# Another order for the first tile's jobs in an attention and SwiGLU kernel

## The chip, the cores and the metric

One core of a Trainium2 chip. The time is that of one execution on the device, in microseconds. The engines are TensorE (PE, matmuls; PEld its weight loads), VectorE (DVE), ScalarE (ACT), GpSimd (POOL), and SyncE (SP), which issues most DMAs; ACT issues the loads of the weights.

## The reference

Attention over 8 batches, 8 heads, 576 positions and head size 64, with keys and values first averaged over groups of 8 positions, then a gated feed-forward layer over all 4608 rows:

```python
k_p = k.reshape(B, H, Sp, 8, D).mean(axis=3)          # Sp = 72
v_p = v.reshape(B, H, Sp, 8, D).mean(axis=3)
scores = scale * np.matmul(q, k_p.transpose(0, 1, 3, 2))
attn = np.exp(scores - np.max(scores, axis=-1, keepdims=True))
attn = attn / (np.sum(attn, axis=-1, keepdims=True) + 1e-09)
x = np.matmul(attn, v_p)                               # then to (4608, 512)
g = x @ w_gate                                         # (512, 1536)
out = (g / (1 + np.exp(-g)) * (x @ w_val)) @ w_out     # (1536, 512)
```

All is float32; q and k are drawn with a spread of 0.8, v with 0.1.

## The kernel before

The 4608 rows are cut into 9 tiles of 512 rows, and the 1536 hidden columns into 12 chunks of 128. To keep float32 accuracy on 16-bit matmuls every operand is split into a high and a low part, and each product is three matmuls (lines 931 to 933). The weights come in 64-bit words, one DMA of 1536 KB for each chunk, and are unpacked and split on the chip once, while tile 0 is computed; after that they stay. Tiles 1 to 8 are run by a planner, which follows its own count of PE's time and puts pieces of attention for later tiles between the matmuls of the current one.

Tile 0 is different. Its work is a list of jobs, ORDER, one name for each, and `first_tile` calls them in that order:

```python
for name in ORDER.split():
    what = name.rstrip("0123456789")
    n = int(name[len(what) :] or 0)
    now["job"] = name
    jobs[what](n)
```

It stands in a manual schedule, so each engine runs its instructions in the order in which the list issues them, and one that waits holds up all behind it on its engine. The engines run beside each other; a job starts when its inputs are there. A DMA that ACT or SP issues is such an instruction too, and waits there until the buffer that it writes is free. The raw tiles (weight words, the first k, and later the "box" of batch 2 and up) share two buffers, and the loads of v, k and q of later batches share three.

The names, with a number for the chunk, piece, step or batch:

- A chunk c of weights: Lw (load, ACT's queue), c (abs, line 244) and b (sign, 231) on ACT, a (ends, 237) and d (join, 248) on DVE, e (sums, 259, ACT), f (total over rows, 209 and 210, PE), g (scale, DVE), h and j (high part of the gate and value weight, ACT; h0, h3 and j1 on POOL), i and k (their low parts, 282, DVE), l (output weight, ACT), m (its low part, 291, POOL), un (factors, POOL).
- Keys and values of batch 0 and 1: Lk, Lv, Lr, Lu (loads, SP), Kp (DVE), Kb and Kq (POOL) sum keys over 8 positions; Vp and Vq sum values (420, PE); Vm, Vo, Vs, Vx, Vh, Vg, Vf scale and split them.
- A piece p of up to 128 rows of attention (0 to 3 are tile 0, 4 to 8 tile 1): Lq (load q), S (scores, 629, PE), M (less the largest, 645 and 646, DVE), E (exponential, 653, ACT), Na (one over the sums, 674 on, DVE), N (normalise, 683, POOL), H and P (high and low part, 696 on ACT, 702 and 703 on POOL), T (a DMA transpose on SP), Y (times values, 747 to 750, PE), R (scale factors, 911 on, DVE), X and Z (high and low part of the rows of x, 770 on ACT and 774 on DVE).
- A hidden step k: G and V (gate and value product, PE), t (tanh, 945, ACT), u and v (949 and 955, DVE), w (copy, 1283, ACT), y (low part, 1287, DVE), O (product with the output weight into the accumulators, 967, PE). Steps 0 to 2 are chunks 0 to 2 for the first 256 rows, 3 to 5 the same chunks for the other 256, and from step 6 on step k is chunk k - 3 for all 512 rows.
- La and Pa: loads and sums for batch 2 (POOL for Pa0 to Pa3, DVE for Pa4 to Pa7).
- ZERO opens the four accumulators with one matmul of zeros each (1246). D with a number issues that many more matmuls of zeros into the first accumulator (1250), I with a number as many into a bank of the gate and value products (1255). They add nothing to the result.

After the list comes O14, the last step's output product, then tile 0 is stored and tile 1 begins.

Of the kernel before, what the change touches and what calls it, by code (L numbers as in the profile page):

```python
# [34 lines left out]


ORDER = """
Lw0 Lk0 Lk1 Lq0 Lv0 Lv2 Kp0 Lv1 Lq1 c0 Kb0 b0 Lu0 a0 CZ Kp1 S0 Lr0 d0 Lq2 M0 l0 Lw1 Vp0
Vp2 E0 Na0 S1 I2 Kq0 e0 f0 Vp1 N0 M1 m0 c1 g0 h0 Vm0 j0 E1 Lq3 Vo0 k0 Vs0 Lu2 I4 H0 Na1
Vx0 Vh0 Vq0 R0 P0 Lr1 Vg0 N1 un0 I5 S2 M2 i0 S3 T0 Kq1 Lu1 H1 Vf0 E2 Y0 Na2 Vq2 X0 Lw2  # L40
Z0 P1 Vq1 b1 M3 Lq4 N2 Vm1 ZERO T1 Vo1 a1 d1 H2 E3 D10 Lw3 Vs1 P2 Vx1 l1 D6 Y1 Vg1 e1 T2
X1 Vh1 m1 R1 c2 f1 D14 g1 Z1 Na3 S4 b2 h1 Lq5 G0 a2 c3 i1 j1 b3 d2 un1 M4 V0 t0 Y2 u0 k1
l2 G1 v0 Lw4 X2 w0 y0 m2 e2 N3 t1 E4 a3 d3 H3 Z2 V1 D8 u1 Lw5 P3 f2 g2 v1 e3 f3 l3 O0 T3
h2 w1 g3 j2 un2 Lq6 c4 i2 G2 y1 m3 k2 j3 V2 h3 b4 t2 i3 Y3 O1 k3 c5 b5 a4 u2 X3 d4 v2 Z3
G3 w2 Vf1 y2 Lw6 V3 t3 O2 a5 d5 u3 v3 e4 f4 l5 Lw7 un3 g4 w3 y3 G4 j4 e5 V4 f5 Na4 O3 k4
t4 h4 c6 u4 v4 w4 N4 g5 l4 S5 y4 G5 m5 i4 M5 H4 b6 t5 u5 V5 v5 O4 P4 G6 Lq7 h5 T4 un4 a6
d6 m4 w5 c7 Lq8 S6 y5 E5 j5 l6 M6 e6 O5 V6 Lw8 Na5 un5 m6 N5 i5 t6 b7 u6 k5 f6 E6 G7 v6
H5 P5 w6 g6 t7 c8 y6 Na6 T5 j6 u7 S7 b8 un6 V7 M7 G8 h6 v7 E7 a7 w7 d7 y7 a8 Y4 Lw9 d8
O6 X4 N6 O7 i6 l7 t8 Z4 e7 Lw10 Y5 e8 V8 k6 X5 l8 m8 u8 m7 c9 Z5 f7 f8 v8 G9 g7 w8 g8
Na7 y8 b9 j7 a9 j8 h7 t9 un7 V9 u9 N7 O8 v9 i7 h8 w9 k7 c10 d9 G10 H7 y9 k8 un8 i8 V10  # L50
La0 t10 e9 f9 l9 u10 O9 v10 m9 P7 g9 Lw11 w10 un9 b10 y10 h9 j9 La1 O10 Pa0 i9 k9 a10
c11 G11 V11 d10 t11 G12 T7 l10 H6 u11 e10 v11 w11 b11 m10 y11 f10 O11 a11 g10 h10 t12
d11 La2 V12 j10 e11 u12 f11 i10 k10 l11 v12 P6 w12 m11 un10 G13 y12 t13 T6 g11 u13 j11
h11 k11 S8 La3 O12 M8 Pa2 un11 i11 La4 V13 E8 Y6 G14 Na8 v13 w13 y13 V14 N8 t14 H8 Ln
Pa3 P8 X6 Pa4 La5 u14 v14 Z6 w14 O13 T8 Y7 X7 Y8 y14 Pa5 Z7 X8 La7 La6 Z8 Pa6 Pa1 Pa7 A
A
"""
HIGH_ON_POOL = ('h0', 'h3', 'j1')
TILE = 512
# [1540 lines left out]
```

## Time and profile before

| | |
|---|---|
| median of 3 runs (lowest, highest) | 938.03 us (937.7, 938.47) |
| span of the profiled execution | 937.0 us |
| PE busy | 901.5 us, 96% |
| DVE busy | 642.8 us, 69% |
| ACT busy | 533.2 us, 57% |
| POOL busy | 439.7 us, 47% |
| first matmul | 11.27 us |
| tile 1's first matmul | 169.58 us |
| weight loads | 12 of 1536 KB, median 6.9 us from issue to landing |

Times of the profile count from the start of the span; 1.0 us of the median lies around it. A matmul's busy time includes its way through the array, so matmuls overlap, and how closely PE is filled is read from the distances between their starts: 0.22 us for one of 512 columns. A row of the timeline has start, duration, engine, line, operation, output and input, shapes and count, and in brackets how long the engine sat idle before it and what released it.

### The profile page before, as it was taken

What the parts mean: (1) busy time and instruction counts of PE and PEld (TensorE: products, weight loads), DVE (VectorE), ACT (ScalarE), POOL (GpSimd) and SP (SyncE); (2) the same over time, 40 slices, a digit from 0 to 9 for tenths busy, and PEclk for the clock granted to TensorE, in tenths of its full rate; (3) what the DMA queues carried; (4) which work ended last, traced back from release to release, by engine and by line L of the source; (5) the groups of instructions that cost most, each with busy time, mean ns of one, the idle gap of its engine ahead of it and who ended that gap; (6) DMA issues with size and microseconds to landing.
All of it is one profiled execution on the core that took longest, in us unless ns stands there. A gap on an engine that the chain in (4) does not pass through costs nothing.

```text
span 937.0 us, 17052 instructions
## 1 busy us (share of the span) xinstructions
PE 901.5 (96%) x6492; PEld 596.1 (64%) x6585; DVE 642.8 (69%) x1163; ACT 533.2 (57%) x1096; POOL 439.7 (47%) x509
## 2 busy tenths in 40 slices
PE   4899999999999999999999999999999999999997
PEld 3667545555445576467757775777577757777775
DVE  5888977886776768777776778667855585644233
ACT  2688774365555455657475655555556656444343
POOL 4654335388856754677366442543124317114111
PEclk9989999999999999999999999999999999999999
DMA  8965733356425633773356334652242321201001
GB/s 332 240 197 174 240 112 110 114 145 179 85 57 149 171 82 56 183 167 88 66 143 185 79 75 129 152 137 41 79 69 63 74 68 24 46 1 46 1 2 45
DMA packets 155538, 103.20 MB, mean 110 GB/s; under 512 B 113216, under 2 KB 141888, under 8 KB 153920
## 3 DMA queue, kind: packets, MB, share of 16 engines
q1 hardware_dynamic: 153728, 83.24, 36.1%
q10 hardware_dynamic: 1728, 18.88, 5.5%
q8 instruction: 51, 0.84, 0.4%
q14 instruction: 31, 0.25, 0.1%
HBM read 67.63 MB, written 9.44 MB: 82 GB/s over the span
## 4 chain that ended last, share of the span: by engine, by line
PE 81%; DVE 6%; DMA 4%; ACT 3%; POOL 3%; issue 2%; SPq 0%; ACTq 0%; DVEq 0%; POOLq 0%
PE gv L1115 29%; PE acc L967 26%; PE gv L931 7%; PE gv L932 7%; PE gv L933 7%; DMA ws<-w_all 2%; PE ps L635 1%; DVE ws L237 1%; PE ps L759 1%; PE ps L636 1%; ACT ws L231 1%; PE ps L760 1%; DMA in<-v_rest 1%; DMA pt<-area 1%; POOL fx L1070 1%
## 5 line engine op out<-in xcount | busy, mean ns | idle before, releaser
L1396 POOL TENSOR_TENSOR hl<-hf,hh 128x512 bf16<-128x512 f32 x71 | 93.2, 1312 | 202.3 <-ACT hh L1387 202.3
L945 ACT ACTIVATE hf<-gv,un 128x512 f32<-128x512 f32 (+1 forms) x111 | 74.8, 674 | 162.7 <-PE gv L1115 110.3
L967 PE MATMUL acc<-hl,wo_h 128*128 128x512 bf16 (+1 forms) x435 | 162.1, 374 | 2.3 <-issue 0.3
L949 DVE SCALAR_TENSOR_TENSOR hf<-hf,gv 128x512 f32<-128x512 f32 (+1 forms) x111 | 74.4, 670 | 115.1 <-ACT hf L945 114.7
L931 PE MATMUL gv<-x,wgv_h 128*128 128x512 f16 (+1 forms) x408 | 149.9, 367 | 1.6 <-ACT x L770 1.0
L932 PE MATMUL gv<-x,wgv_h 128*128 128x512 f16 (+1 forms) x408 | 149.8, 367 | 0.5 <-DVE x L774 0.5
L933 PE MATMUL gv<-x,wgv_l 128*128 128x512 f16 (+1 forms) x408 | 149.7, 367 | 0.0
L967 PE MATMUL acc<-hh,wo_h 128*128 128x512 f32 (+1 forms) x444 | 130.2, 415 | 0.0
L967 PE MATMUL acc<-hb,wo_l 128*128 128x512 bf16 x307 | 117.2, 382 | 0.4
L1115 PEld LDWEIGHTS <-mixed 128*128 128x128 f16 x1044 | 101.3, 98 | 25.5 <-issue 0.9
L618 POOL TENSOR_TENSOR box<-qt,box 64x512 f16<-64x512 f32 (+1 forms) x60 | 66.3, 1104 | 107.1 <-ACT box L617 93.6
L1115 PEld LDWEIGHTS <-wgv_h 128*128 128x128 f16 x960 | 92.9, 98 | 34.0 <-issue 2.1
L1387 ACT CAST hh<-hf 128x512 fp32r<-128x512 f32 x72 | 44.4, 617 | 119.8 <-DVE hf L955 119.8
L1115 PE MATMUL gv<-area,mixed 128*128 128x256 f16 x696 | 94.9, 273 | 0.0
L1115 PE MATMUL gv<-x,wgv_h 128*128 128x256 f16 x528 | 93.0, 273 | 0.0
L967 PEld LDWEIGHTS acc<-hh,wo_h 128*128 128x128 f32 x444 | 76.4, 190 | 13.7 <-ACT hh L1387 0.3
L955 DVE SCALAR_TENSOR_TENSOR hf<-gv,un,hf 128x512 f32<-128x512 f32 x72 | 53.8, 747 | 37.0 <-PE gv L1115 34.5
L967 PEld LDWEIGHTS <-wo_l 128*128 128x128 bf16 x444 | 43.4, 98 | 52.3 <-issue 25.4
L1115 PE MATMUL gv<-x,wgv_l 128*128 128x256 f16 x264 | 72.0, 273 | 0.0
L933 PEld LDWEIGHTS <-wgv_l 128*128 128x128 f16 x408 | 40.0, 98 | 43.8 <-issue 0.7
L932 PEld LDWEIGHTS <-wgv_h 128*128 128x128 f16 x408 | 40.0, 98 | 39.9 <-issue 2.0
L931 PEld LDWEIGHTS <-wgv_h 128*128 128x128 f16 x408 | 40.6, 99 | 38.5
(206 smaller groups left out, 1917.6 us busy)
## 6 DMA issues: line engine op xcount, KB each, us to landing
ws<-w_all ACTq DMA_DIRECT2D x12, 1536.0 KB, 6.9
qt<-q_twice SPq DMA_DIRECT2D x48, 256.0 KB, 3.0
out_t<-ob SPq DMA_DIRECT2D x36, 256.0 KB, 2.5
in<-k_rows SPq DMA_DIRECT2D x12, 576.0 KB, 5.0
in<-q_rows SPq DMA_DIRECT2D x12, 576.0 KB, 4.9
in<-v_main SPq DMA_DIRECT2D x12, 512.0 KB, 4.9
in<-v_rest SPq DMA_DIRECT2D x12, 512.0 KB, 4.8
qt<-q_rows SPq DMA_DIRECT2D x8, 256.0 KB, 6.4
```

What stands on the lines that cost most here:

```text
L231: nc.scalar.activation(high.bitcast(I32), high.bitcast(F32), AF.Prelu, scale=2.0**-18, alpha=2.0**90)
L618: nc.gpsimd.tensor_sub(o[rows], qt[rows], o[rows])
L931: nc.tensor.matmul(o, wh, x["h"][:, j, a:e], start=(j == 0), stop=False)
L932: nc.tensor.matmul(o, wh, x["l"][:, j, a:e], start=False, stop=False)
L933: nc.tensor.matmul(o, wl, x["h"][:, j, a:e], start=False, stop=(j == NJ - 1))
L945: nc.scalar.activation(hf, gate, AF.Tanh, scale=un[:, c, 0:1])
L949: nc.vector.scalar_tensor_tensor(out=hf, in0=hf, scalar=1.0, in1=gate, op0=ALU.add, op1=ALU.mult)
L955: nc.vector.scalar_tensor_tensor(out=out, in0=val, scalar=un[:, c, 2:3], in1=hf, op0=ALU.mult, op1=ALU.mult)
L967: nc.tensor.matmul(acc[j][:, a:e], w[:, c, j * P : (j + 1) * P], h[:, :n], start=begin and at < NJ, stop=end and w is wo_up,)
L1115: nc.tensor.matmul(o, a, b, start=begin and j + n == 0, stop=j == HJ - 1 and n == 2, skip_group_check=True,)
L1387: nc.scalar.copy(hh[:, :n], hf)
L1396: eng.tensor_sub(hl[:, :n], hf, hh[:, :n].bitcast(F32))
```

## The change

Only the list changes. All jobs but D6, D8, D10 and D14 are in it as before, in another order under the same dependencies and buffers; the four D jobs (38 zero matmuls) are left out, and ZERO and the three I jobs stay. Lines of the changed kernel are numbered two lower than before. The first and a later line of each list:

```diff
-Lw0 Lk0 Lk1 Lq0 Lv0 Lv2 Kp0 Lv1 Lq1 c0 Kb0 b0 Lu0 a0 CZ Kp1 S0 Lr0 d0 Lq2 M0 l0 Lw1 Vp0
...
-X1 Vh1 m1 R1 c2 f1 D14 g1 Z1 Na3 S4 b2 h1 Lq5 G0 a2 c3 i1 j1 b3 d2 un1 M4 V0 t0 Y2 u0 k1
+Lw0 c0 CZ Lk0 Lv0 Lk1 Vp0 Lq1 Kb0 Kp0 b0 Lw1 Kp1 Lq0 a0 S1 Lv2 S0 d0 Lv1 e0 Vp1 M1 f0 E1 M0 E0
...
+ZERO T2 S4 d2 b3 Kq0 M4 Lw4 e2 E4 l2 a3 un1 G0 m1 f2 Y3 j1 g2 V0 d3 t0 u0 X3 h2 Y2 i1 G1 j2 e3
```

Three places matter below. First, ScalarE's queue around the load of chunk 2 (L225 DMA, tile ws_386). Before, from V's scaling (L450) on:

```order
L450 ACTIVATE area_120<-ps_183,inv_122 64x4x64 x2
L696 CAST area_120<-sc_237 128x512
L698 CAST area_120<-sc_237 128x2x32 x2
L472 ACTIVATE area_120<-shapes_91,mask_92 128x2x64 x4
L653 ACTIVATE sc_323<-sc_323 128x576
L770 ACTIVATE x_289<-ps_355,r_296 128x4x128
L225 DMA ws_386<-w_all 128x3072
L231 ACTIVATE ws_181<-ws_181 128x1536
```

Now (there it is L223, tile ws_287), from chunk 1's abs (L242) and sign (L229) on:

```order
L242 ACTIVATE mixed_111<-ws_159 128x1536
L229 ACTIVATE ws_159<-ws_159 128x1536
L223 DMA ws_287<-w_all 128x3072
L448 ACTIVATE area_120<-ps_143,inv_122 64x4x64 x2
L694 CAST area_120<-sc_200 128x512
L696 CAST area_120<-sc_200 128x2x32 x2
```

The load has moved from behind the attention work of the first pieces, and ahead of chunk 1's sign, to right behind that sign.

Second, VectorE's queue around the first hidden step (u0 is L949 on hf_577, before; chunk 3's ends and join are L237 and L248 on ws_440):

```order
L949 SCALAR_TENSOR_TENSOR hf_577<-hf_577,gv0_537 128x256
L282 SCALAR_TENSOR_TENSOR wgv_l_108<-mixed_111,sw_514,wgv_h_107 128x512
L955 SCALAR_TENSOR_TENSOR gv1_564<-gv1_564,un_125,hf_577 128x256
L1287 TENSOR_TENSOR hl_618<-gv1_564,hh_616 128x256
L237 SCALAR_TENSOR_TENSOR ws_440<-ws_440 128x1536
L248 SCALAR_TENSOR_TENSOR mixed_111<-mixed_111,ws_440 128x1536
```

Now (u0 is L947 on hf_570, chunk 3 is ws_405):

```order
L235 SCALAR_TENSOR_TENSOR ws_405<-ws_405 128x1536
L213 TENSOR_SCALAR p2w_113<-ps_532 128x2
L216 RECIPROCAL sw_553<-p2w_113 128x2
L246 SCALAR_TENSOR_TENSOR mixed_111<-mixed_111,ws_405 128x1536
L947 SCALAR_TENSOR_TENSOR hf_570<-hf_570,gv0_518 128x256
L280 SCALAR_TENSOR_TENSOR wgv_l_108<-mixed_111,sw_438,wgv_h_107 128x512
L953 SCALAR_TENSOR_TENSOR gv1_556<-gv1_556,un_125,hf_570 128x256
```

Chunk 3's two long operations have moved from behind the first hidden step to ahead of it.

Third, GpSimd's queue around P6, the low part of piece 6 (L702 and L703 on half_123 from sc_1022, before), and the sums Pa of batch 2 (L301 to L303):

```order
L357 MEMSET box_1437 128x2x4x72
L301 TENSOR_TENSOR in_1381<-in_1381 128x2x256
L302 TENSOR_TENSOR in_1381<-in_1381 128x2x128
L303 TENSOR_TENSOR box_1437<-in_1381 128x128
L291 TENSOR_TENSOR wo_l_110<-mixed_111,wo_h_109 128x512
L702 TENSOR_TENSOR half_123<-sc_1022,half_123 128x512
```

Now, from Pa2 (in_776, the second of four) on:

```order
L299 TENSOR_TENSOR in_776<-in_776 128x2x256
L300 TENSOR_TENSOR in_776<-in_776 128x2x128
L301 TENSOR_TENSOR box_1413<-in_776 128x128
L299 TENSOR_TENSOR in_1058<-in_1058 128x2x256
L300 TENSOR_TENSOR in_1058<-in_1058 128x2x128
L301 TENSOR_TENSOR box_1413<-in_1058 128x128
L299 TENSOR_TENSOR in_1246<-in_1246 128x2x256
L300 TENSOR_TENSOR in_1246<-in_1246 128x2x128
L301 TENSOR_TENSOR box_1413<-in_1246 128x128
L700 TENSOR_TENSOR half_123<-sc_983,half_123 128x512
```

Three more of batch 2's sums have moved ahead of P6.

More of the change, by code (lines that the diff above doesn't have):

```diff
@@ L37 @@
 ORDER = """
-Lw0 Lk0 Lk1 Lq0 Lv0 Lv2 Kp0 Lv1 Lq1 c0 Kb0 b0 Lu0 a0 CZ Kp1 S0 Lr0 d0 Lq2 M0 l0 Lw1 Vp0
-Vp2 E0 Na0 S1 I2 Kq0 e0 f0 Vp1 N0 M1 m0 c1 g0 h0 Vm0 j0 E1 Lq3 Vo0 k0 Vs0 Lu2 I4 H0 Na1
-Vx0 Vh0 Vq0 R0 P0 Lr1 Vg0 N1 un0 I5 S2 M2 i0 S3 T0 Kq1 Lu1 H1 Vf0 E2 Y0 Na2 Vq2 X0 Lw2
-Z0 P1 Vq1 b1 M3 Lq4 N2 Vm1 ZERO T1 Vo1 a1 d1 H2 E3 D10 Lw3 Vs1 P2 Vx1 l1 D6 Y1 Vg1 e1 T2
-X1 Vh1 m1 R1 c2 f1 D14 g1 Z1 Na3 S4 b2 h1 Lq5 G0 a2 c3 i1 j1 b3 d2 un1 M4 V0 t0 Y2 u0 k1
-l2 G1 v0 Lw4 X2 w0 y0 m2 e2 N3 t1 E4 a3 d3 H3 Z2 V1 D8 u1 Lw5 P3 f2 g2 v1 e3 f3 l3 O0 T3
@@ L44 @@
[L44 to L55, printed above, removed]
@@ L56 @@
-A
+Lw0 c0 CZ Lk0 Lv0 Lk1 Vp0 Lq1 Kb0 Kp0 b0 Lw1 Kp1 Lq0 a0 S1 Lv2 S0 d0 Lv1 e0 Vp1 M1 f0 E1 M0 E0
+Vp2 Lq2 Na1 Lu0 Vm0 g0 I4 Na0 Lq3 Vo0 S2 S3 Vs0 c1 b1 R0 Lw2 a1 Vx0 Vq0 Vh0 N1 N0 H1 h0 P1 Vg0
+H0 I2 Lu2 Vf0 M3 d1 c2 Lq4 M2 P0 Lu1 Vq2 Vq1 i0 T0 e1 E3 Na3 j0 Vm1 T1 Y0 N3 un0 Lr1 E2 X0 Lr0
+Z0 Lw3 Lq5 Vo1 l0 H3 I5 Na2 b2 Vs1 m0 k0 N2 f1 Vg1 g1 Vx1 Y1 P3 H2 T3 a2 X1 P2 l1 h1 Vh1 c3 Z1
+ZERO T2 S4 d2 b3 Kq0 M4 Lw4 e2 E4 l2 a3 un1 G0 m1 f2 Y3 j1 g2 V0 d3 t0 u0 X3 h2 Y2 i1 G1 j2 e3
+v0 k1 Lw5 X2 w0 V1 Lq6 i2 t1 G2 y0 Z3 O0 c4 u1 un2 Na4 f3 Kq1 Z2 b4 t2 l3 v1 G3 u2 m2 k2 w1 g3
@@ new lines @@
+c5 V2 y1 O1 a4 N4 t3 G4 V3 u3 b5 v2 w2 d4 y2 Lw6 a5 t4 La2 e4 O2 v3 u4 w3 H4 f4 d5 y3 j3 e5 g4
+Lq7 h3 G5 t5 V4 m3 f5 i3 j4 O3 un4 k3 La0 h4 Lw7 v4 g5 S5 un3 P4 w4 T4 l4 c6 b6 k4 y4 i4 u5 un5
+m4 M5 V5 v5 G6 a6 S6 l5 w5 E5 h5 V6 O4 y5 t6 j5 d6 M6 u6 G7 c7 Na5 v6 k5 m5 b7 Lw8 e6 i5 f6 g6
+w6 N5 t7 y6 u7 O5 V7 La1 Vf1 S7 G8 a7 v7 O6 H5 P5 c8 d7 h6 b8 w7 a8 t8 V8 Lw9 y7 l6 E6 d8 M7 j6
+e8 O7 u8 m6 Lq8 i6 un6 l8 f8 v8 e7 w8 k6 y8 c9 g8 R1 Na6 f7 b9 g7 Lw10 V9 T5 G9 a9 j7 E7 l7 d9
+t9 m8 u9 h7 La3 e9 Y4 O8 f9 Lw11 j8 m7 i7 v9 N6 g9 k7 w9 G10 Na7 y9 X4 h8 i8 Y5 k8 c10 un7 V10
@@ L57 @@
+t10 N7 O9 b10 u10 un9 a10 v10 La4 c11 G11 h9 un8 w10 La7 i9 V11 b11 Pa0 La6 H6 j9 y10 d10 a11 Z4
+G12 H7 t11 l10 e10 f10 Pa2 X5 u11 v11 t12 d11 Pa1 w11 Z5 O10 e11 g10 u12 h10 j10 f11 y11 l11 k9
+Pa3 k10 i10 V12 g11 h11 P6 v12 l9 S8 un10 T6 M8 w12 G13 P7 Ln V13 m9 t13 E8 Y6 O11 m10 X6 y12
+i11 j11 Na8 N8 H8 T7 u13 m11 v13 Y7 Pa4 P8 G14 T8 X7 w13 Pa6 k11 La5 Pa7 un11 t14 y13 O12 Z6 u14
+V14 Y8 O13 v14 w14 X8 Z7 y14 Z8 Pa5 A A
 """
```

## Prediction

> **What bounds the kernel now.** I read the page's slices first, then TensorE's waits, then its start times around the first tile, then VectorE.
>
> ```profile
> PE   4899999999999999999999999999999999999997
> ...
> PE gv L932 <- DVE x L774: 0.5, 1, 0.5
> ```
>
> PE is busy in every slice, but busy counts pipelined matmuls, the zero matmuls too. The second row is the whole answer of the waits view for PE from 73.7 to 169 us: one wait of 0.5 us. So from about 73 us on the PE queue is full, and whatever the first tile loses it loses before. The starts show where:
>
> ```profile
> 72.83 0.27 PE L931 MATMUL gv<-x,wgv_h 128*128 128x256 f16 x1 [1.00 <-ACT x L770]
> 73.62 0.27 PE L932 MATMUL gv<-x,wgv_h 128*128 128x256 f16 x1 [0.52 <-DVE x L774]
> ...
> 117.46 0.38 PE L931 MATMUL gv<-x,wgv_h 128*128 128x512 f16 x1
> ...
> 169.58 0.38 PE L931 MATMUL gv<-x,wgv_h 128*128 128x512 f16 x1
> ```
>
> At 72.83 PE waits for the last time, for the x rows of the second half tile; at 117.46 it begins job V9, the value half of chunk 6; at 169.58 it begins tile 1. Behind that the matmuls stay the same, so the change is worth what it moves 169.58. And what feeds PE is VectorE:
>
> ```profile
> 8.85:112.10 103.25, 88.60 (x157) 0.97 0.74 230
> ```
>
> Columns: window, its length, DVE's busy time and instructions. From its first real work at 8.85 until it has finished k6 (the low part of chunk 6's value weight, V9's last input, at 112.1) DVE is busy 88.60 of 103.25 us and idles 14.65. That idle time is what an order can win back. Its largest piece by line and releaser:
>
> ```profile
> DVE hl L1287 <- ACT hh L1283: 2.1, 4, 1.1
> ```
>
> That is four waits, the longest 1.1 us; the rest is spread as thinly, over a dozen lines.
>
> **The change, part by part.**
>
> *The 38 zero matmuls (D8, D6, D10, D14).*
>
> ```profile
> 39.38 3.61 PE L1250 MATMUL acc<-zeros 128*128 128x512 f16 x16
> 46.21 4.87 PE L1250 MATMUL acc<-zeros 128*128 128x512 f16 x14
> 59.06 1.89 PE L1250 MATMUL acc<-zeros 128*128 128x512 f16 x8
> ```
>
> They take 10.4 us of PE, the last ending at 60.95. All lie ahead of the last wait at 72.83, so I cost their removal at nothing: the cover is the wait for x. What they may do for the clock is a rival below. ZERO (four matmuls that open the accumulators) and the hums I2, I4, I5 stay.
>
> *The same work for PE.* No useful matmul is added or dropped. If V9 starts at time s in the new order, tile 1 starts at s plus the PE work behind V9. Before that was 169.58 - 117.46 = 52.1 us. In the new list G9 (before: ahead of V9), Y4 and Y5 stand behind it. G9 is 12 matmuls 0.22 us apart, 2.6 us; Y5 took from 110.56 to 111.47, 0.9 us, and Y4, half as wide, 0.5:
>
> ```profile
> 110.56 0.22 PE L747 MATMUL ps<-pt,area 128*128 128x128 f16 x1
> 111.47 0.38 PE L931 MATMUL gv<-x,wgv_h 128*128 128x512 f16 x1
> 112.28 0.22 PE gv L931
> 112.50 0.22 PE gv L932
> ```
>
> Nothing that was behind V9 is now ahead of it, so 52.1 + 4.0 = 56.1 us.
>
> *The same work for VectorE, up to k6.* The new list has R1, Na6 and Z4 behind k6 (before: ahead), and u8, v8 ahead of it (before: behind).
>
> ```profile
> 45.66 0.22 DVE L911 TENSOR_TENSOR top<-p2s 128x1 f32<-128x1 f32 x1
> 46.79 0.16 DVE L215 TENSOR_SCALAR p2w<-ps 128x2 uint32<-128x2 uint32 x1
> 79.07 0.73 DVE L674 TENSOR_REDUCE sm<-sc 64x8 f32<-64x576 f32 x1
> 80.15 0.69 DVE L282 SCALAR_TENSOR_TENSOR wgv_l<-mixed,sw,wgv_h 128x512 f16<-128x512 f32 x1
> L774 DVE SCALAR_TENSOR_TENSOR x<-ps,r,x 128x256 f16<-128x256 f32 x1 | 0.5, 479 | 0.0
> L949 DVE SCALAR_TENSOR_TENSOR hf<-hf,gv 128x512 f32<-128x512 f32 x3 | 2.0, 665 | 0.0
> L955 DVE SCALAR_TENSOR_TENSOR gv<-gv,un,hf 128x512 f32<-128x512 f32 x2 | 1.5, 752 | 0.3 <-PE gv L933 0.3
> ```
>
> R1 is 46.79 - 45.66 = 1.13, an Na 80.15 - 79.07 = 1.08, Z4 0.48; u8 0.67, v8 0.75. So 88.60 - 2.69 + 1.42 = 87.3 us of work. With DVE waits W from 8.85 on, V9's input is ready at 96.2 + W, and
>
> tile 1 starts at 8.85 + 87.3 + 56.1 + W = 152.3 + W.
>
> At the old idle time, W = 14.65, that is 166.9. Everything hangs on W.
>
> *The weight loads.* In the old list the load of chunk 2 stands behind X0 on ScalarE's queue and goes out at 34.12, though its buffer is free after d0 at 16.8. In the new one it stands right behind b1.
>
> ```profile
> 15.05 1.74 DVE L248 SCALAR_TENSOR_TENSOR mixed<-mixed,ws 128x1536 uint32<-128x1536 uint32 x1
> 16.91 0.33 ACTq L225 DMA_DIRECT2D ws<-w_all  x1
> 24.61 1.61 ACT L244 ACTIVATE mixed<-ws 128x1536 f32<-128x1536 f32 x1 [4.16 <-DMA ws<-w_all]
> 34.12 0.34 ACTq L225 DMA_DIRECT2D ws<-w_all  x1
> ws<-w_all ACTq DMA_DIRECT2D x12, 1536.0 KB, 6.9
> ```
>
> Load 1 now waits only for k's pooling (Kp1, Kb0), about 13.5 us, and by the old 24.61 - 16.91 = 7.7 lands near 21.2; abs and sign take 3.2, so load 2 leaves near 24.5 and lands near 32, and chunk 3 follows near 45. In exchange PE's S0 starts behind S1 and v's second half of k lands third in SP's queue. SP's order is otherwise only shifted; its transposes stand behind loads as before.
>
> ```profile
> 18.54 0.68 ACT L653 ACTIVATE sc<-sc 128x576 f32<-128x576 f32 x1 [1.10 <-DVE sc L646]
> 19.13 0.61 ACT L259 ACTIVATE wgv_h<-mixed 128x512 f16<-128x512 f32 x1
> ...
> 20.27 0.19 ACT L259 ACTIVATION_READ_ACCUMULATOR wgv_h<-mixed 128x1 f32 x1
> ```
>
> These are an exponential (E, 0.7) and one chunk's sums (e, from 19.13 to 20.46, 1.3). I then walked the new lists of VectorE and ScalarE job by job: a job starts when its engine is free and its inputs are there, with the durations above and their like. DVE is fed almost without a break from 12 us on: chunk 3's ends and join (a3, d3) stand ahead of the first hidden step at about 49 to 53, where the old order had them at 57.6 to 61. Waits that I find: 2.2 us before Na3, because E3 stands behind c2 and e1 on ScalarE and c2 waits for load 2 (32 + 1.6 + 1.3 + 0.7 = 35.6 against 33.4); 2 us before a8, because load 8 can leave only behind b7 at about 86, lands at 93, and c8, h6, b8 take 4; and five of 0.3 to 1.0 at Kp1, a1, a3, y0 and u3, together 3.3 with their neighbours. That makes 7.5. A walk has no short hand-overs; the old list has some 3 us of them in the same stretch (14.65 less the waits that the view names, 11.7). So W = 10.5 and tile 1 starts at 162.8, 6.8 us earlier. The bounds of W: 5 (half of what I found, and the hand-overs) and 14.65.
>
> *Places behind V9* can only push it later. V12 (k9 ends 27 us of DVE work behind k6, V12 stands 29 us of PE work behind V9) has 2 us to spare, and two sign waits in between. Y6 I sum below at 143.4, with 18.7 us of PE work from there on: 162.1, nearly the same. I add 1.5 us for both: 164.3, or 5.3 less than 169.58.
>
> *Tiles 1 to 4.* The planner's clock starts otherwise, so pieces of later tiles move by a slot. PE's longest waits there show what can be lost or won:
>
> ```profile
> PE ps L635 <- POOL box L618: 1.2, 1, 1.2
> PE gv L1115 <- DVE gv L1488: 0.7, 1, 0.7
> ```
>
> I take 0, bounds 2 us either way.
>
> The profiled execution's span is 937.0; the median of the runs is 938.03, so 1.0 lies around it. 938.03 - 5.3 = 932.7.
>
> **Rivals.**
>
> *As many waits as now.* W = 14.65 and the same 1.5: 168.4, the kernel takes 936.8. For it: every row of a wait above is a hand-over between engines that no order abolishes. Against: load 2 leaves 10 us earlier.
>
> *TensorE slower without the zeros.*
>
> ```profile
> 64.27 0.41 PE L967 MATMUL acc<-hl,wo_h 128*128 128x256 bf16 x1
> 64.47 0.42 PE L967 MATMUL acc<-hh,wo_l 128*128 128x256 bf16 x1
> ...
> 64.00:68.00 4.00, 4.00 (x26) 0.63 1.00 317
> ```
>
> In this window PE's granted clock is 0.63, and 256-wide matmuls stand 0.20 us apart, against 0.11 at full clock (half of the 0.22 above). It follows the thin stretch from 60.6 to 63.2. Without zeros the new order is thinner still: PE has little between Y1 near 37 and G0 near 46.5. From G0 to O1 stand 14.6 us of PE work; at half clock all the way it would cost 14.6 more, but most of it falls into waits that are there anyway. Bounds 0 and 7; as a case of its own 4: tile 1 at 168.3, the kernel at 936.7.
>
> [...]
>
> *GpSimd's queue (the other side).* In the new list the four sums Pa0, Pa2, Pa1, Pa3 stand together ahead of P6; before only Pa0 did. Pa0 opens with a memset of a buffer that holds a weight chunk until d10.
>
> ```profile
> 29.09 0.30 POOL L703 TENSOR_TENSOR half<-sc,half 128x64 f16<-128x64 f32 x1
> 33.00 0.22 PE L747 MATMUL ps<-pt,area 128*128 128x128 f16 x1 [0.21 <-DVE sc L646]
> 136.69 0.58 POOL L357 MEMSET box<- 128x576 f16 x1 [5.58 <-DVE mixed L248]
> 139.80 1.28 POOL L291 TENSOR_TENSOR wo_l<-mixed,wo_h 128x512 bf16<-128x512 f32 x1
> 141.03 1.17 POOL L702 TENSOR_TENSOR half<-sc,half 128x512 f16<-128x512 f32 x1
> ```
>
> Memset and one sum take 139.80 - 136.69 = 3.1, so all four 0.6 + 4 x 2.5 = 10.6; P6 1.5; from its end to the first matmul on the turned block 33.00 - 29.39 = 3.6. d10 ends about 21 us behind k6, at 127.7, so Y6 can start at 143.4. Behind that point stand Y6 to Y8 (0.9 each), G14 and V14 (2.6 each) and O11 to O14 (2.7 each): 18.7. Tile 1 moves later than now from a Y6 of 150.9 on, and the kernel is slower by 0.2% from 152.8 on. The way there: Pa3's input can be loaded only when an earlier sum has freed one of three buffers. If it goes out behind Pa1 instead of Pa0, the sums wait some 5 us (Y6 at 148.3, kernel 936); with the same wait for Pa1's own input Y6 is at 153.3, tile 1 at 172.0, the kernel at 940.4. For it: the place is in all three queues (POOL, SP, the buffers) at once. Against: the inputs of Pa0, Pa2 and Pa1 leave far ahead.
>
> *Fewer waits.* W = 5 and nothing behind V9: tile 1 at 157.3, the kernel at 925.8.
>
> **How the numbers follow.** 0.2% of the kernel, 1.9 us, is about what a measurement of it can tell from no change. Chances: my forecast (W from 8 to 13) 0.58, all of it faster; as many waits as now 0.14, half of it faster by over 0.2%, half the same; the slower clock 0.09, likewise halved; GpSimd's queue 0.11, of which 0.02 ends within 0.2% and 0.09 slower; fewer waits 0.08, faster. Faster 0.58 + 0.07 + 0.04 + 0.08 = 0.77, same 0.07 + 0.05 + 0.02 = 0.14, slower 0.09. The range: W = 7 with 1.5 and tiles 1 to 4 gaining 1 gives 928; at the other end no change plus half a microsecond, 938.5. My forecast alone would reach from 929.5 to 936.
>
> **What the profile of the changed kernel would show.** Right: tile 1's first matmul near 164; DVE idle near 10 us between its first sum over k and k6, and k6 near 107; load 2 leaving near 24.5; chunk 3's join ending near 53; PE waiting a few tenths of a us at several value steps up to V9 instead of once at 72.8; 38 zeros fewer and nothing missing for it. Wrong: a PE clock well under 1 beyond 60 us; a PE wait of microseconds at Y6 for the turned block, with POOL waiting for a load ahead of P6; DVE idle 14 us or more ahead of k6, which would leave the time where it is; or PE waits in tiles 1 to 4 of over 2 us together that are not there now.

## The result, and the profile after

The changed kernel is slower: 944.61 us (median of 4 runs, 942.8 to 945.32) against 937.99 for the kernel before beside it, a ratio of 1.0069 with an interval of 1.0054 to 1.0083. In a second comparison it took 942.52 against 938.14, 1.0046 (1.0033 to 1.0059). The profile of that second comparison was of a disturbed execution and is not read; all that is read of the changed kernel below is from the first, whose span is 943.2 us. The forecast was 932.7.

Where does the time go? First by tiles: SP's first store of a tile marks its end. Before:

```profile
169.23 5.68 SPq L1127 DMA_DIRECT2D out_t<-ob  x4
...
380.46 2.20 SPq L1127 DMA_DIRECT2D out_t<-ob  x4
473.84 1.83 SPq L1127 DMA_DIRECT2D out_t<-ob  x4
```

After:

```profile
171.24 1.81 SPq L1125 DMA_DIRECT2D out_t<-ob  x4
...
380.41 2.50 SPq L1125 DMA_DIRECT2D out_t<-ob  x4
480.27 2.16 SPq L1125 DMA_DIRECT2D out_t<-ob  x4
```

The first tile, the only one whose code was changed, ends 2.0 us later by this mark. Tiles 1 and 2 win that back (380.41 against 380.46). Then tile 3 takes 99.86 us instead of 93.38, and from there the distance stays: of the 6.4 us at 480.27, all stand in a tile that the change does not touch.

Second, the first tile's own path. VectorE from its first real work to the end of k6 (window, length, busy time and count):

```profile
8.85:108.09 99.24, 93.02 (x148) 0.91 0.77 245
```

It idles 6.2 us there instead of 14.65, less than forecast; but its busy time is 93.0 where 87.3 was forecast. Then TensorE's starts, and its longest row in the waits view from 73.7 to 175 us (before, that view was one row of 0.5 us):

```profile
108.83 0.38 PE L929 MATMUL gv<-x,wgv_h 128*128 128x512 f16 x1 [1.41 <-DVE hl L1285]
147.74 0.59 PE L929 MATMUL gv<-x,wgv_h 128*128 128x512 f16 x1 [2.09 <-DVE hl L1285]
170.62 0.38 PE L930 MATMUL gv<-x,wgv_h 128*128 128x512 f16 x1
```

```profile
PE gv L929 <- DVE hl L1285: 4.0, 3, 2.1
```

```profile
108.09 0.69 DVE L1285 TENSOR_TENSOR hl<-gv,hh 128x512 bf16<-128x512 f32 x1
```

V9 starts at 108.83, 8.6 us earlier than before. What releases it is not k6 but y8 (L1285, the last row above), which stands right behind k6 on VectorE and ends 0.7 us later. V13 waits at 147.74, and tile 1's matmuls run in a row from 170.62 (one slips in at 169.54, ahead of the last of O14), 1.0 later than the 169.58 of before. From V9 to there it takes 61.8 us, where the 52.1 of before and the 4.0 of work that the list moved there gave 56.1. So the lead is there at V9 and gone at tile 1. Third, TensorE's longest waits behind 175 us; before, the longest was 1.2 us:

```profile
PE ps L757 <- DMA pt<-area: 2.4, 1, 2.4
PE acc L965 <- POOL hl L1394: 1.6, 2, 1.4
PE gv L1113 <- DVE hf L953: 1.2, 2, 1.0
PE ps L745 <- DMA pt<-area: 1.1, 1, 1.1
PE ps L633 <- DVE sc L644: 1.0, 1, 1.0
```

The 2.4 us stand at the start of tile 3. In the windows (PE's, PEld's, DVE's, ACT's and POOL's busy time, then the granted clock and the DMA share) low clocks follow the waits:

```profile
108.00:112.00 4.00, 3.17 (x11) 1.30 (x11) 3.65 (x17) 3.85 (x5) 0.00 (x0) 0.77 0.37 83
148.00:152.00 4.00, 4.00 (x13) 1.48 (x12) 2.21 (x5) 0.00 (x0) 4.00 (x4) 0.61 1.02 209
388.00:392.00 4.00, 1.69 (x19) 1.14 (x20) 1.52 (x3) 0.47 (x1) 3.28 (x4) 0.76 0.95 250
392.00:396.00 4.00, 4.00 (x17) 1.72 (x16) 1.43 (x3) 1.30 (x2) 0.00 (x0) 0.82 0.00 0
```

### The profile page after: what moved, and what is told of

Same layout as the page of the kernel before. It is cut to its first block, busy times and chain, and to the rows that moved or that the text cites. A ratio compares the mean times of both kernels' runs of the same rounds, so it can differ in the third digit from the quotient of the medians.

```text
span 943.2 us, 17065 instructions
## 1 busy us (share of the span) xinstructions
PE 908.3 (96%) x6547; PEld 597.5 (63%) x6547; DVE 649.7 (69%) x1163; ACT 533.5 (57%) x1096; POOL 454.2 (48%) x509
## 4 chain that ended last, share of the span: by engine, by line
PE 76%; POOL 6%; DVE 6%; DMA 5%; issue 3%; ACT 2%; SPq 0%; POOLq 0%; DVEq 0%; ACTq 0%
PE gv L1113 27%; PE acc L965 26%; PE gv L929 6%; PE gv L930 6%; PE gv L931 6%; DMA ws<-w_all 2%; DMA k<-k_rows 1%; DMA pt<-area 1%; POOL in L299 1%; POOL box L616 1%; DVE wgv_l L280 1%; PE ps L633 1%; DVE mixed L246 1%; PE ps L757 1%; POOL in L300 1%
## 5 line engine op out<-in xcount | busy, mean ns | idle before, releaser
L943 ACT ACTIVATE hf<-gv,un 128x512 f32<-128x512 f32 (+1 forms) x111 | 75.0, 676 | 171.5 <-PE gv L1113 108.1
L965 PE MATMUL acc<-hl,wo_h 128*128 128x512 bf16 (+1 forms) x444 | 164.3, 373 | 1.6 <-POOL hl L1394 1.6
L929 PE MATMUL gv<-x,wgv_h 128*128 128x512 f16 (+1 forms) x408 | 152.1, 373 | 5.5 <-DVE hl L1285 5.1
L947 DVE SCALAR_TENSOR_TENSOR hf<-hf,gv 128x512 f32<-128x512 f32 (+1 forms) x111 | 74.3, 670 | 120.0 <-ACT hf L943 119.8
L930 PE MATMUL gv<-x,wgv_h 128*128 128x512 f16 (+1 forms) x408 | 152.1, 373 | 0.0
L965 PE MATMUL acc<-hb,wo_l 128*128 128x512 bf16 x384 | 146.5, 382 | 0.0
L616 POOL TENSOR_TENSOR box<-qt,box 64x512 f16<-64x512 f32 (+1 forms) x60 | 70.1, 1169 | 117.8 <-ACT box L615 96.6
```

What stands on the lines that cost most here:

```text
L616: nc.gpsimd.tensor_sub(o[rows], qt[rows], o[rows])
L929: nc.tensor.matmul(o, wh, x["h"][:, j, a:e], start=(j == 0), stop=False)
L930: nc.tensor.matmul(o, wh, x["l"][:, j, a:e], start=False, stop=False)
L943: nc.scalar.activation(hf, gate, AF.Tanh, scale=un[:, c, 0:1])
L947: nc.vector.scalar_tensor_tensor(out=hf, in0=hf, scalar=1.0, in1=gate, op0=ALU.add, op1=ALU.mult)
L965: nc.tensor.matmul(acc[j][:, a:e], w[:, c, j * P : (j + 1) * P], h[:, :n], start=begin and at < NJ, stop=end and w is wo_up,)
```

## The experiments

Theory: two losses that have nothing to do with each other. In the first tile GpSimd's four sums ahead of P6 give back what the order wins up to V9; in tile 3 the planner's order, made from another state at the list's end, puts a transpose behind stores. Rivals: the missing zeros and the clock; the first tile alone, whatever comes later.

**The zeros alone.** The kernel before, its list without D10, D6, D14 and D8.

> The kernel before with its 38 zero matmuls (D10, D6, D14, D8) left out and every other row of every engine unchanged. Theory (the zeros stand in time in which TensorE would wait, and the loss of the change comes from elsewhere): 938.0 us within 1.0. Rival (without the zeros TensorE's clock is granted late and the first tile's matmuls run slower): 939.5 to 943, with a granted clock below that of the kernel before in the stretch behind 44 us.

938.8 us against 938.46, ratio 1.0002 (0.9994 to 1.0011): no change. The mean granted clock of its runs is lower, 0.990 to 0.993 against 0.994 to 1.0, but the time does not follow it: from 40 to 72 us the granted clock is 0.73 against 0.89 before, and tile 1's first matmul comes at 169.93, 0.35 us later. For the old list the rival falls; no run puts these zeros back into the new list.

**The list and the planner's state, apart.** At the end of the list the planner goes on from its own clocks. The old list leaves GpSimd's at 94.3 us of the planner's count (Pa1 stands at the very end), the new one at 75.3; TensorE's is 91.9 in both. `prep` lets the next batch's sizes go on only when TensorE's clock has passed GpSimd's, so with the new list they go on at once, and all pieces of tiles 1 to 4 take other slots. The numbers can be set by hand:

```diff
             for name in ORDER.split():
+                if name == "A":
+                    now.update({"V": 91312.0, "A": 89862.0, "P": 94264.0})
+                    freed[:] = [0, 0, 0, 65428.0, 83788.0, ..., 91312.0]
```

With that the changed kernel's rows from tile 1 on are those of the kernel before on every engine; setting "P" alone gives the same rows. The mirror is the old list with the new list's numbers.

> The changed kernel, but at the end of the list the planner's clocks and the times of freed buffers are set to the numbers that the old list leaves, so that tiles 1 to 8 are issued in the order of the kernel before on every engine. Theory (about 6 us of the loss are lost in tiles 1 to 4, by the order that the planner makes from another starting state; the first tile by itself costs 1 to 2 us): 938.5 to 940.0 us, with tile 3 back at 93.4 us. Rival (the first tile or the data and buffers that it leaves are the cause, whatever the later order): 943 to 945 us, tile 3 near 99.8.

> The kernel before with its own list, but the planner starts the later tiles from the numbers that the new list leaves, so that tiles 1 to 8 are issued in the order of the changed kernel. Theory (the later order is the larger part of the loss): tiles 1 and 2 about 2 us shorter, tile 3 about 6.4 longer, 942.0 to 943.8 us in all. Rival (first tile): 937.5 to 938.5 us. If the two parts add up, this run and the new list with the old start together show the whole 6.6 us.

The new list with the old start took 936.58 against 938.46, 0.9976 (0.9965 to 0.9988); once more, in the set below, 0.999 (0.9981 to 0.9999). So it is 1 to 2 us faster than the kernel before, below the 938.5 to 940.0 us expected, and the later order costs the changed kernel 5.4 us (942.52 against 937.17) to 8.0 (944.61 against 936.58). These times hold the first tile too, where the granted clock differs from one execution to the next under the same list: it is low behind V9 and V13 in the changed kernel's profile (8 us at 0.77 and 0.80, 4 us at 0.61, some 3.3 us in all), behind V13 alone in the second profile of the new list with the old start (4 us at 0.61), and behind neither in the first. Counted from tile 1's run of matmuls to the end of the span, the changed kernel takes 772.6 us (943.2 less 170.62) and the new list with the old start 765.6 and 766.0 (932.9 less 167.33, 935.3 less 169.35): without the first tile the later order costs 6.6 to 7.0 us. Tile 3 is back at 93.28 us (its ends at 376.96 and 470.24 in the first profile). The old list with the new start took 951.49, 1.0139 (1.0126 to 1.0152), far above the 943.8 expected. Tile 3 is 100.0 long there too, with a wait of 3.0 us at the same place; but tile 1 grew by 7.3 us, since the sizes now go on at the end of a list whose sums are not done (the waits end at 176.06 and at 397.74 us):

```profile
PE ps L210 <- DVE mx L361: 4.0, 1, 4.0
...
PE ps L759 <- DMA pt<-area: 3.0, 1, 3.0
```

The two parts therefore do not add up; what both runs with the new start share is tile 3.

**Tile 3's wait.** SP's queue around tile 2's stores (at 380.46 and 380.41 above): before, the row ahead of them; after, the row ahead of them and the two behind:

```profile
377.55 1.83 SPq L738 DMA_TRANSPOSE pt<-area  x1
```

```profile
378.43 1.89 SPq L736 DMA_TRANSPOSE pt<-half  x1
...
382.97 0.78 SPq L495 DMA_DIRECT2D in<-v_main  x1
383.91 4.29 SPq L736 DMA_TRANSPOSE pt<-area  x1
```

The transpose of `area` has moved behind the four stores and a load (ahead of the stores now stands that of `half`), although GpSimd had finished its source at 380.15, and its issue takes 4.3 us instead of 1.8. The experiment issues tile 2's stores behind it:

```diff
-                nc.sync.dma_start(out=out[...], in_=ob[:, j % 2])
+                late_out.append(lambda ob=ob, j=j: nc.sync.dma_start(out=out[...], in_=ob[:, j % 2]))
+        if lo != 2 * TILE:
+            send_late()
...
         t["pt"] = turned(m, half, OLD // P if b < SPLIT else 2 * H)
+        send_late()
```

> The changed kernel with one edit on SP's queue: tile 2's four stores are issued behind the next transpose (pt<-area) instead of ahead of it; every other row of every engine is unchanged. Theory (the transpose stands behind the stores, which makes TensorE wait 2.5 us at 387.6 and run at a clock of 0.76 and 0.82 for the 8 us behind, some 1.7 us): the wait is gone or under 0.5 us, tile 3 at 94.5 to 96.5 us, 939 to 941.5 us in all. Rival (the transposes are late because of the DMA traffic there, a share of 1.1 of the engines from 380 to 388 us, or the values' place in TensorE's order is too early for any transpose): the wait stays within 1 us, 943 to 945 us.

939.64 us, 1.002 (1.0011 to 1.003), beside 942.52 for the changed kernel on the same chip: 2.9 of the 4.4 us that the changed kernel lies above the kernel before in that comparison. Counted from the end of tile 1 (278.03 there, 280.89 changed) the transpose is issued 2.9 us earlier, and TensorE's wait is 0.26 instead of 2.35:

```profile
378.18 3.79 SPq L736 DMA_TRANSPOSE pt<-area  x1
382.08 2.39 SPq L1132 DMA_DIRECT2D out_t<-ob  x4
384.79 0.20 PE L757 MATMUL ps<-box,pt 128*128 128x64 f16 x1 [0.26 <-DMA pt<-area]
```

The granted clock is 1.00 from 380 to 400 us. The issue itself still takes 3.8 us with the stores behind it, so they are not what makes it long; the load of v stands ahead of it in both, and whether that is the reason no run shows. The tiles' border moves with the stores, so tiles 2 and 3 are taken together: 195.35 us against 199.38 changed and 193.61 before. In these profiles the order of SP's queue is 4.0 of the 5.8 us. The 1.7 that stay fit TensorE's other waits in the two tiles (1.0, 0.3, 0.2 and 1.0 us, against 0.7 and 0.4 before); no experiment takes those away.

**GpSimd's queue in the first tile.** In the changed kernel d10 ends at 130.0 and the four sums hold GpSimd until P6:

```profile
130.12 0.58 POOL L355 MEMSET box<- 128x576 f16 x1 [5.58 <-DVE mixed L246]
...
144.34 1.15 POOL L700 TENSOR_TENSOR half<-sc,half 128x512 f16<-128x512 f32 x1
145.46 0.31 POOL L701 TENSOR_TENSOR half<-sc,half 128x64 f16<-128x64 f32 x1
```

```profile
145.80 0.45 DVE L644 TENSOR_TENSOR sc<-ps,mx 64x288 f32<-64x288 f32 x1 [2.34 <-POOL half L701]
...
147.02 0.67 DVE L1285 TENSOR_TENSOR hl<-gv,hh 128x512 bf16<-128x512 f32 x1
```

M8 on VectorE needs the score buffer that P6 reads, so it waits 2.34 us; y12 (L1285) stands behind it in VectorE's queue; V13 needs the bank that y12 reads. Two experiments, both with the old start: P6 and T6 ahead of all four sums (P7 and T7 move forward too, P7 behind the first sum; the sums' loads and the VectorE sums Pa4 to Pa7 move back), and the opposite, P6 four times in a row.

```diff
-... Pa0 La6 H6 ... Pa2 X5 ... Pa1 w11 ... Pa3 k10 i10 V12 g11 h11 P6 v12 l9 S8 un10 T6 M8 ...
+... H6 ... P6 X5 u11 v11 t12 d11 T6 w11 Z5 O10 Pa2 La3 ... P7 Pa0 La4 ... un10 M8 w12 G13 T7 Pa1 ...
```

> The changed kernel with the old starting state for tiles 1 to 8, and with GpSimd's four batch sums (Pa0, Pa2, Pa1, Pa3), their loads and the VectorE sums of the same batch moved behind P6 and T6 in the list. Theory (the new list is 5 us ahead when TensorE has passed V9, and the four sums ahead of P6 give that back through M8, y12, V13 and Y6): TensorE's first matmul of tile 1 at 164 to 166 us, 932.0 to 935.0 us in all, below both kernels. Rival (the gain up to V9 is lost at the next wait whatever GpSimd does: DVE's or ACT's work on the last chunks is late by itself): 937 to 940 us, as the new list with the old start. Second rival (the moved sums and loads are late for tile 1): first matmul near 165, but tiles 1 or 2 longer by over 2 us.

> The list with the sums behind P6, old start, once more beside the list with the sums ahead of it: if what GpSimd's queue takes back is 1 to 3 us, this one is 1 to 3 us below it, 933.5 to 935.5 us; if the 1.1 us between them in the first comparison were chance, within 0.7 us of it.

> The new list with the old start, with P6's two GpSimd operations issued four times in a row instead of once (the same values are written again): about 4.4 us more on GpSimd (three times 1.46 us) ahead of un10, P7, T6's transpose and the release of M8's buffer; no other row changes. Theory (GpSimd's queue sets when V13 and tile 1 start): the wait ahead of V13 grows by 3 to 4.4 us and the time with it, 939.5 to 941.5 us against 936.6 for the same list with P6 once. Rival (DVE or ACT is late there by itself): within 1.5 us of that.

> The new list with the old start once more, as the base for the two beside it on the same chip: 935.5 to 937.5 us, a ratio to the kernel before of 0.997 to 0.999.

The sums behind P6: 935.44, 0.996 (0.9946 to 0.9974), and once more 933.87, 0.995 (0.9937 to 0.9963), 3.3 us below the new list beside it (937.17). It beats both kernels. P6 four times: 942.33, 1.0047 (1.0035 to 1.006), 5.2 above the list with P6 once, a little more than expected. The same two places there:

```profile
148.13 0.45 DVE L644 TENSOR_TENSOR sc<-ps,mx 64x288 f32<-64x288 f32 x1 [7.11 <-POOL half L701]
150.08 0.59 PE L929 MATMUL gv<-x,wgv_h 128*128 128x512 f16 x1 [6.83 <-DVE hl L1285]
```

4.1 us more on GpSimd make V13 wait 4.1 us more than the 2.7 of the same list with P6 once; the other 1.1 us stand beside a low clock behind it (0.50 and 0.71 from 148 to 156). GpSimd's queue sets V13's start one for one. With the sums behind P6 the longest wait from 130 to 170 us is 0.8 us, and from V9 (110.32 and 110.00) to tile 1's run of matmuls (167.72 and 167.50) it takes 57.4 and 57.5 us, against 59.2 (108.11 to 167.33) and 60.9 (108.43 to 169.35, with V13's low clock) with the sums ahead and 61.8 in the changed kernel. Tile 1 does not start at the 164 to 166 expected, because V9 itself is some 2 us later in both runs than with the sums ahead. The lists are alike up to V9, and why it comes later no run shows: TensorE waits 3.5 us for the first queries in one of the two, but only 1.5 in the other, as in the changed kernel.

**That list with its own start.**

> The list with GpSimd's four batch sums behind P6 and T6, now with the planner's starting state as that list leaves it, which gives tiles 1 to 8 the changed kernel's order. Theory (the first tile and the later order add up): 1 to 3 us below the changed kernel and 6.5 to 8.5 us above the same list with the old start (935.4), so 941.5 to 943.5 us, tile 3 near 99.8. Rival (the old start was what made the moved sums cheap): 944 us or more.

947.76 us, 1.0102 (1.009 to 1.0114): the rival's side. Tile 3 is 98.56 long, a little less than expected: TensorE waits 2.4 us at its start again, but the clock behind stays at 1.00. Tile 1 grew by 8 us over the same list with the old start, for the same reason as with the old list: the sums now stand at the list's end while the planner has counted them as done, and TensorE waits for the sizes:

```profile
PE ps L208 <- DVE mx L359: 4.6, 1, 4.6
```

**Zeros in the waits, and the changed kernel once more.** D6 ahead of V9 and D9 ahead of V13.

```diff
-... g7 Lw10 V9 ... w12 G13 P7 Ln V13 ...
+... g7 Lw10 D6 V9 ... w12 G13 P7 Ln D9 V13 ...
```

> The changed kernel with 6 zero matmuls (of 0.216 us each) into an accumulator ahead of V9 and 9 ahead of V13, to lie in TensorE's waits of 1.5 and 2.3 us there; no other row changes. Theory of the clock (short waits are followed by a low granted clock, which cost tile 0 of the changed kernel up to 3.3 us): granted clock 1.00 from 100 to 160 us and 941.5 to 943.5 us. Rival (the clock does not follow these waits, or the dips were chance): within 1 us of the changed kernel run beside it; the zeros themselves cost under 0.5 us, as they stand in waits.

> The changed kernel once more, without an edit, beside the three below on the same chip, for a second profile. If the stretches of low granted clock behind TensorE's short waits at V9 (0.77 and 0.80 from 108 to 116 us) and V13 (0.61 from 148 to 152) are chance, they come at other waits or not at all this time, and tile 0 ends up to 3 us earlier; the loss in tile 3 (99.85 us against 93.38 before) is in the order and comes back within 1 us. Time 943 to 945.5 us.

The changed kernel once more took 942.52 us, a little under what was expected, and with the zeros in its waits 942.91: no difference. The clock is 1.00 from 100 to 124 and from 140 to 160 us, as the clock's theory said, but a gain of 1 to 2 us is not in the medians. Nor does the profile settle it: there V9 starts at 110.81, 2.0 us later than in the changed kernel, and was late before the zeros. What a low window costs can be read from the traces: from V13 to tile 1's run of matmuls it takes 22.9 us in the two executions with a low window there (147.74 to 170.62 changed, 146.43 to 169.35 in the second with the old start) and 21.3 in two without (148.96 to 170.21 here, 146.08 to 167.33), so 1.6 us. How often it comes no run shows. Tile 3's wait, unfilled, is again followed by low windows:

```profile
108.00:112.00 4.00, 4.00 (x24) 2.30 (x23) 3.86 (x14) 2.48 (x4) 0.20 (x1) 1.00 0.01 2
...
388.00:392.00 4.00, 2.22 (x20) 1.40 (x21) 1.22 (x2) 0.08 (x1) 3.27 (x4) 0.71 0.80 224
```

**Why VectorE was busy longer.** In the new list (here with the old start) some of VectorE's long operations are stretched. Two of the joins (L246, 1.75 us in the list before), each of which starts while a GpSimd operation runs, and GpSimd at those times:

```profile
82.16 2.50 DVE L246 SCALAR_TENSOR_TENSOR mixed<-mixed,ws 128x1536 uint32<-128x1536 uint32 x1
99.42 2.83 DVE L246 SCALAR_TENSOR_TENSOR mixed<-mixed,ws 128x1536 uint32<-128x1536 uint32 x1
```

```profile
80.41 2.64 POOL L289 TENSOR_TENSOR wo_l<-mixed,wo_h 128x512 bf16<-128x512 f32 x1 [1.29 <-ACT wo_h L286]
99.36 1.28 POOL L289 TENSOR_TENSOR wo_l<-mixed,wo_h 128x512 bf16<-128x512 f32 x1 [4.31 <-ACT wo_h L286]
```

The experiment takes six of those GpSimd operations away:

```diff
     def w_out_low(c):
+        if 1 <= c <= 6:
+            return
```

> The new list with the old start, without GpSimd's six subtractions for the low part of chunks 1 to 6's output weights (m1 to m6, L289, 1.3 us each); this leaves a part of the computation out: those low parts are zero, filled once at the start while GpSimd idles. No row of another engine changes. Theory (VectorE's operations with two SBUF inputs are held up while a GpSimd operation runs: L246 takes 2.2 to 2.9 us beside one and 1.75 alone, and five of the stretched ones up to k6 stand beside an m job, together 4.2 us): VectorE's busy time from 8.85 us to the end of k6 falls from 93.7 by 3 to 5 us, k6 ends 2 to 5 us earlier than 107.4, and the kernel takes 932 to 935.5 us against 936.6 and 937.2. Rival (they are long for another reason, DMA traffic or ACT beside them): busy time within 1 us of 93.7 and 936 to 938 us.

```profile
82.36 1.75 DVE L247 SCALAR_TENSOR_TENSOR mixed<-mixed,ws 128x1536 uint32<-128x1536 uint32 x1
99.91 1.75 DVE L247 SCALAR_TENSOR_TENSOR mixed<-mixed,ws 128x1536 uint32<-128x1536 uint32 x1
```

Both joins are at 1.75 again, so the GpSimd operation beside them is the cause. In all VectorE's busy time up to k6 falls from 93.45 to 90.96, 2.5 us and not 3 to 5: at some places another GpSimd operation takes the empty slot (the join at 52.0 still takes 2.15). k6 ends only 0.6 us earlier, as VectorE's idle time grows by 1.9, and the kernel takes 935.58, 0.997 (0.9958 to 0.9983), which overlaps both runs of the list with those operations. The stretch is shown; that it costs the kernel time is not.

## Why the prediction was wrong

*Tiles 1 to 4, "I take 0, bounds 2 us either way"*: the step that failed. The later order costs 5.4 to 8.0 us by the medians and 6.6 to 7.0 without the first tile; waits of over 2 us together in those tiles, a sign of being wrong that the forecast had named, are there. The bounds came from the longest waits of the old order (1.2 and 0.7 us), and those say nothing of what another order puts side by side: one transpose behind four stores made a wait of 2.4 us, with a clock of 0.76 and 0.82 behind it in this execution, and with smaller waits tile 3 is 6.5 us longer. That the planner's clock would start otherwise was said; what the queues then hold at the borders of tiles was not looked at.

*Places behind V9, "I add 1.5 us for both"*: the second step, a term too small. V9 to tile 1 took 5.7 us more than the 56.1 of work in the changed kernel, and 3.1 and 4.8 more in the two profiles of the new list with the old start. With the sums behind P6 it is 1.3 and 1.4, so the term would have held but for GpSimd's queue.

*GpSimd's queue*, the rival with 0.11: right in its place, too small in its chance, and not right in its path. Y6 came at 151.98 instead of 143.4, beyond the 150.9 from which it was to decide, and with the 18.7 us of work from there on tile 1 is due at 170.7; measured is 170.6. That this agrees is partly luck: Y6 came right behind V13, and without the low clock there (1.6 us) it would have stayed ahead of 150.9. d10 ended at 130.0 instead of 127.7 and the four sums took 13.7 us (130.66 to 144.34) instead of 10, some of their operations being longer than others of the same shape (2.16 and 1.26 us, 2.13 and 0.73). The wait ended elsewhere than told: not at Y6 for the transpose, but already at V13, by way of M8 and y12, and not because POOL waited for a load.

*VectorE up to k6*: near in the sum, by the luck of two opposite errors. W was 6.2 and not 10.5; the work was 93.0 and not 87.3, because the forecast took each operation at its duration in the old order; of the 5.7 us between them 2.5 went away with six GpSimd operations, and what makes up the rest no run shows. k6's end came at 108.1 instead of 106.7. That k6 is "V9's last input" was a misreading: V9 also needs y8, which is what it waited for. The weight loads did what was forecast:

```profile
23.43 0.33 ACTq L223 DMA_DIRECT2D ws<-w_all  x1
...
52.47 2.72 DVE L246 SCALAR_TENSOR_TENSOR mixed<-mixed,ws 128x1536 uint32<-128x1536 uint32 x1
```

Load 2 left at 23.4 (forecast 24.5), and chunk 3's join ended at 55.2 (forecast 53), one of the stretched ones.

*The 56.1 us behind V9*: right as a sum of work; 57.4 us were left where GpSimd's queue was out of the way. In the changed kernel 108.83 + 56.1 = 164.9, and the 5.7 us on top are V13's wait of 2.1 and the low clocks of some 3.3.

*The zeros cost nothing*: right for the old list, 1.0002; *TensorE slower without them*: right there that the clock falls (0.73 against 0.89), wrong as a price. Zeros do not always go with a high clock: before, the 14 from 46.21 take 0.35 us each, at 0.81 and 0.77 from 44 to 52 us, and the 16 from 39.38 take 0.23, at 1.00 from 40 to 44. In the new list neither was tested.

*The first tile as a whole*: forecast -5.3; the new list with the old order behind it gives -1.0 and -1.9, with the sums moved behind P6 -3.0 and -4.3. The direction was right, and 1 to 3 us of what was missing were GpSimd's queue. The rest fits V9, which comes at 110.3 and 110.0 with the sums moved instead of 106.7; what makes it vary is open.

## What to carry to other kernels

When a list ends in a planner, read the state that it leaves (here one number, GpSimd's clock) and compare the queues behind it row by row, above all the DMA queue at borders where stores are issued; a list that is faster by itself can lose more there than it won. An operation moved off the critical path still has a place in its own engine's queue: ask which buffer the next one in that queue releases, and who stands behind the one that needs it.

## What the runs showed of the hardware

The join L246 on VectorE took 0.75 and 1.08 us longer than its 1.75 where GpSimd's L289 was under way as it started (2.50 at 82.16 and 2.83 at 99.42), and 1.75 at both places without L289. L289 still had 0.89 and 1.22 us to run (until 83.05 and 100.64), 0.14 more than the join lost in both. That is no measure for other operations: in the run without six of the L289 the join at 52.01 lost 0.40 us beside GpSimd's L274, which still had 1.41 to run (until 53.42). Whether it matters that the join has two inputs in SBUF, as the expectation has it, no run shows.

Short waits of TensorE were followed by a lower granted clock in some executions and not in others. The new list with the old start has the same wait of 2.70 us ahead of V13 in both profiles; the clock behind it (the third number from the end of each second row) is 1.00 in the first and 0.61 in the second:

```profile
146.08 0.38 PE L929 MATMUL gv<-x,wgv_h 128*128 128x512 f16 x1 [2.70 <-DVE hl L1285]
148.00:152.00 4.00, 3.92 (x30) 2.51 (x30) 3.70 (x6) 2.10 (x5) 4.00 (x5) 1.00 0.86 210
```

```profile
146.43 0.38 PE L929 MATMUL gv<-x,wgv_h 128*128 128x512 f16 x1 [2.70 <-DVE hl L1285]
148.00:152.00 4.00, 4.00 (x24) 2.46 (x23) 2.38 (x5) 0.21 (x1) 4.00 (x5) 0.61 0.92 214
```

Likewise V9's wait of 1.41 us in the changed kernel is followed by 0.77 and 0.80, and one of 1.26 us in the new list with the old start by 1.00; tile 3's of 2.35 us by 0.76 and 0.82 in the changed kernel, and one of 2.37 us by 1.00 in the list with the sums behind P6 and its own start. So waits of 1.41 to 2.70 us stand ahead of a clock of 0.61 to 0.82, and waits of 1.26 to 2.70 us ahead of 1.00; what decides between them no run shows.
